# Batch 0 of a fused attention and mixer kernel: later panels and side blocks, a later z transpose, and relus shared between two engines

## The chip, the cores and the metric

The kernel runs on one core of a Trainium2 chip. The metric is the device time in microseconds (us) of one execution; lower is better. Engines are named as in the profile: PE is TensorE, PEld its weight load, DVE is VectorE, ACT is ScalarE, POOL is GpSimd, SP is SyncE, whose queue issues the transposing DMAs.

## The reference, cut to what matters

```python
scores = (1 / S) * z @ z.T             # 8 batches, S = 3136, z is S x 64
attn   = maximum(scores, 0) ** 2       # symmetric: scores of (o, j) and (j, o) are each other's transpose
x      = u * (attn @ v)                # D = 256
y      = x + (x.T @ U @ V).T           # rank 32
out    = y + maximum(y @ w1, 0) @ w2   # 256 -> 1024 -> 256
```

## The kernel before

S is cut into 25 tiles of 128. `A[j]` holds 13 of the 25 blocks of panel j; the other 12 blocks that an output o needs are the transposes of blocks in panel o itself, and come as a *strip* from one transposing DMA. So for every output tile o the order is: score matmul, relu with scale on ACT, square on DVE, transpose by DMA, and only then can PE use the strip. The *side blocks* of the start are those blocks of panels 8 to 15 that outputs 20 and later need.

```python
def score(b, parts):                        # parts: up to two pieces, each of at most 512 columns
    ps = pair_psum()                        # one PSUM tile of two banks
    ...                                     # one 64-row matmul per bank, the two side by side
    for dst, src in todo:
        nc.scalar.activation(out=dst, in_=src, func=AF.Relu, scale=sc)
    for dst, _ in todo:
        nc.vector.tensor_tensor(out=dst, in0=dst, in1=dst, op=ALU.mult)

def turn(b, o):                             # the strip; five buffers
    strip = strip_pool.tile([P, HALF, P], BF16, name="strip")
    transpose(out=strip, in_=A[o][:, P:])   # nc.sync.dma_start_transpose
    strips[b, o] = strip
```

Batches 1 to 7 find their panels half made by the batch before. Batch 0 finds nothing, so it has a start of its own: outputs 12 to 15 with half-made panels, then 16 to 19 (the "tail" of the start makes what is missing for outputs 20 and later), then the main loop over outputs 20, 21, 22, 23, 24, 0, 1, ... 11. The main loop calls an output "step i", where step 8 is output 20, step 12 is output 24, step 13 is output 0.

```python
# the start, cut
rest = []                                                    # side blocks for outputs 20 and later
for j in reversed(range(FIRST - NG, LEAD)):
    rest += score_steps(0, j, LEAD + NG - j, NB)             # 8 steps
more = [s for j in range(LEAD + NG, LEAD + 2 * NG - 1) for s in score_steps(0, j)]   # panels 20, 21, 22
for i, pair in enumerate(pairs):
    ...
    if B > 1 and i in (1, 2):                                # z of batch 1: doubled by DVE, turned by DMA
        part = ((0, FIRST), (FIRST, NF))[i - 1]
        double_z(1, (part,))
        turn_z(1, (part,))
    if i == len(pairs) - 1:
        turn(0, LEAD + NG)                                   # strip 20, in the same queue
...
# the main loop, cut: what is made in step i, and which strips are turned after it
first_at    = {8: [panel 23, panel 0], 9: [panel 24], 10: [panel 1, ...], 11: [panel 2, ...], 12: [...]}
first_turns = {8: (23,), 9: (24, 0)}                         # from step 10 on: the strip of step i + 4
```

Of the kernel before, what the change touches and what calls it, by code (L numbers as in the profile page):

```python
# [10 lines left out]
ALU = mybir.AluOpType  # L11
# [31 lines left out]
def kernel(  # L43
# [11 lines left out]
    nc = tc.nc  # L55
# [136 lines left out]
    def turn_z(b, parts):  # L192
        z_bf = z_tiles[b]
        for t0, t1 in parts:
            transpose(
                out=zT_of(b)[:, t0 : upto(t1), :],
                in_=z_bf[:, t0 : upto(t1), :, :].rearrange("p t h c -> p (t h c)"),
            )
# [90 lines left out]

    strips = {}  # L290

    def score(b, parts):

        ps = pair_psum()
        zT = zT_of(b)
        zT_flat = zT.rearrange("p t c -> p (t c)")
        for k, (j, c, n, _) in enumerate(parts):
            mm(  # L298
                out=ps[:, k, :n],
                lhsT=zT[halves[k], j, :],  # L300
                rhs=zT_flat[halves[k], c : c + n],
                start=True,
                stop=True,
            )
        if parts[0][3] is parts[-1][3]:
            n = parts[0][2]
            todo = [(parts[0][3], ps[:, :, :n] if len(parts) == 2 else ps[:, 0, :n])]
        else:
            todo = [(part[3], ps[:, k, : part[2]]) for k, part in enumerate(parts)]
        for dst, src in todo:  # L310
            nc.scalar.activation(out=dst, in_=src, func=AF.Relu, scale=sc)  # L311
        for dst, _ in todo:
            nc.vector.tensor_tensor(out=dst, in0=dst, in1=dst, op=ALU.mult)  # L313

    def score_steps(b, j, k0=0, k1=NB):
        steps = []
        n = (k1 - k0) * P
        parts = _ceil_div(n, 1024)
        each = n // parts
        h = each // 2  # L320
        for i in range(parts):
            at = k0 * P + i * each

            def step(at=at):
                dst = A[j][:, at : at + each].rearrange("p (i h) -> p i h", i=2)
                score(b, [(j, j * P + at + i * h, h, dst) for i in range(2)])

            steps.append(step)
        return steps
# [329 lines left out]
    def beside(o, j, w, stop=(False, False)):  # L659
        t0, _ = pair_of(o)  # L660
        for h in range(1 if j == NF else 2):
            half(0, o, j, h, w, (t0, h) not in begun, stop[h], skip_group_check=True)
            begun.add((t0, h))

    def start_up():
        parts = ((8, 16), (0, 8), (16, NF))
        first_z(parts[:2])
# [34 lines left out]
        where = {}  # L702
        mark = small.tile([P, D], BF16, name="mark", tag="t1_sb")[:1, :8]

        def make(pair):
            if all(LEAD - 1 - HALF <= j < FIRST for j in pair):
                todo = []
                for j in pair:
                    at = (FIRST - j) * P
                    where[j] = A[j][:, at : at + NG * P]  # L710
                    todo.append((j, c0, NG * P, where[j]))
                score(0, todo)
            else:
                room = rooms.pop(0)
                for i, j in enumerate(pair):
                    where[j] = room[:, i, :]
                score(0, [(j, c0, NG * P, room) for j in pair])

        def use(pair, some):
            for j in pair:  # L720
# [5 lines left out]
        for i, pair in enumerate(pairs):  # L726
            if i == 5 and B > 1:

                nc.sync.dma_start(out=mark, in_=v_both[1][:1, V_PARTS[2][1] - 1, :8])
            if i == 3:  # L730
                double_z(0, parts[2:])
            if i == 5:
                turn_on_pe([(16, NF)], [pair_psum().rearrange("p a w -> p (a w)")])
                turn_on_pe([(NF, NT)], [pair_psum()[:, 0, :]])
                extend_z(0)
            make(pair)
            if i > 5 and i % 2:
                nxt.pop(0)()
            if i > 1:
                use(pairs[i - 2], outs)  # L740
# [16 lines left out]
                    if 0 <= o - j <= HALF:  # L757
                        beside(o, j, block(0, o, j))

        def make_stored(pair):  # L760
            todo = []
            for j in pair:
                k0, k1 = LEAD - j, min(NB, LEAD + NG - j)
                todo.append((j, LEAD * P, (k1 - k0) * P, A[j][:, k0 * P : k1 * P]))
            score(0, todo)

        nxt += [lambda pair=pair: make_stored(pair) for pair in pairs[:2]]
        run(nxt[:2])
        own = [
            lambda j=j, some=some: use_stored([j], some)  # L770
# [2 lines left out]
            if j <= some[-1]  # L773
        ]
        run(_merge(nxt[2:], own))
        rest = []
        for j in reversed(range(FIRST - NG, LEAD)):
            rest += score_steps(0, j, LEAD + NG - j, NB)
        more = [s for j in range(LEAD + NG, LEAD + 2 * NG - 1) for s in score_steps(0, j)]
        for i, pair in enumerate(pairs):  # L780
            if i + 2 < len(pairs):
                make_stored(pairs[i + 2])
            else:
                more.pop(0)()
            use_stored(pair, outs)
            if B > 1 and i in (1, 2):
                part = ((0, FIRST), (FIRST, NF))[i - 1]
                double_z(1, (part,))
                turn_z(1, (part,))
            if i == len(pairs) - 1:  # L790
                turn(0, LEAD + NG)
        tail = []
        for o in outs:
            js = [(o + 1 + i) % NT for i in range(HALF)]

            def close(o=o, j=js[-1]):
                beside(o, j, block(0, o, j), [o % 2 == 1] * 2)
                if o % 2:
                    close_pair(0, o)
                if o == outs[1]:  # L800
                    load_u(0, LEAD + NG)
                if o < outs[-2]:
                    turn(0, o + NG + 1)

            for i in range(3):
                some = js[4 * i : min(4 * i + 4, HALF - 1)]
                tail.append(lambda o=o, js=some: [beside(o, j, block(0, o, j)) for j in js])
            tail.append(close)
# [8 lines left out]
    for j, i in enumerate((6, 7, 8, 9, 3, 5, 4, 2, 9, 8, 7, 6)):  # L817
        own_at[i].append((j, 0, FIRST - j))

    first_at = {8: [(NT - 2, 0, NB), (0, 0, NB)], 9: [(NT - 1, 0, NB)], 10: [(1, 0, NB)]}  # L820
    first_at.update({11: [(2, 0, NB)], 12: []})
    for j, i in zip(range(3, FIRST), (10, 11, 11, 12, 12, 12, 12, 12, 12)):
        first_at[i].append((j, 0, FIRST - j))
    first_turns = {8: (NT - 2,), 9: (NT - 1, 0)}

    next_at = {i: [] for i in range(NT)}
    for j in range(FIRST):
        next_at[max(NB, FIRST + j)].append((j, FIRST - j, NB))
    for j, i in enumerate((14, 15, 16, 18, 19, 20, 24)):
        next_at[i].append((FIRST + j, 0, NB))  # L830

    def run(steps):
        for s in steps:
# [6 lines left out]
    for b in range(B):  # L840
# [7 lines left out]
        for i in range(begin, NT):  # L848
            o = turns(i)
            fill = [s for key in own.get(i, ()) for s in score_steps(b, *key)]  # L850
            if more:
                fill += [s for key in next_at[i] for s in score_steps(b + 1, *key)]
                if b and i == 1:
                    load_z(b + 1, WHOLE)
                if b and i == 7:
                    turn_z(b + 1, ((FIRST, NF),))
                if b and i == 10:
                    turn_z(b + 1, ((0, FIRST),))
                if b == 0 and i in v_at:
                    load_v(b + 1, v_at[i])  # L860
                if i == 11:
                    extend_z(b + 1)
            main = attend_steps(b, o)
            if b and i in ahead:
# [80 lines left out]
```

## Time and profile before

| | before |
|---|---|
| time, median of 3 runs | 1003.15 us (999.58 to 1004.6) |
| span of the profiled run | 998.3 us |
| PE busy | 983.4 us |
| batch 0's own stretch (first attention matmul to the first of batch 1) | 94.2 us |

Two lines of the page of before: busy time by engine (first part) and the chain that ended last (fourth part).

```profile
PE 983.4 (99%) x13688; PEld 776.5 (78%) x13688; DVE 551.1 (55%) x1003; ACT 612.2 (61%) x835; POOL 171.7 (17%) x317
...
PE 91%; DVE 4%; ACT 3%; DMA 1%; issue 1%; POOL 0%; DVEq 0%; POOLq 0%
```

PE is nearly always busy and makes up 91% of the chain that ended last. There is little to gain except where PE is idle. The next view is the busy time of each engine in stretches of 10 us, with the granted PE clock, the share of the 16 DMA engines (packet time over the time of 16 engines, which can exceed 1) and GB/s.

```profile
core 0: us, PE busy (x) PEld busy (x) DVE busy (x) ACT busy (x) POOL busy (x), PEclk, DMA share, GB/s
20.00:30.00 10.00, 8.06 (x104) 5.46 (x103) 8.41 (x15) 9.51 (x15) 2.61 (x5) 1.00 1.03 179
40.00:50.00 10.00, 6.91 (x114) 5.58 (x111) 6.88 (x15) 7.38 (x13) 1.61 (x3) 1.00 1.19 200
60.00:70.00 10.00, 9.45 (x169) 6.70 (x166) 7.79 (x18) 7.61 (x16) 2.66 (x4) 1.00 1.22 208
70.00:80.00 10.00, 10.00 (x181) 8.54 (x176) 7.96 (x14) 8.01 (x11) 0.58 (x1) 1.00 1.30 204
80.00:90.00 10.00, 10.00 (x176) 8.37 (x172) 8.38 (x16) 7.84 (x11) 3.50 (x5) 1.00 1.18 186
```

PE has free time up to 70 us and none in the two rows after it. Which wait it is, the table of waits of PE between 16 and 95 us says (total us, how many, longest):

```profile
PE ps L371 <- DMA strip<-A: 2.5, 1, 2.5
PE ps L298 <- ACT A L311: 2.3, 4, 0.7
PE ps L371 <- DVE A L313: 2.0, 4, 0.9
```

The largest single wait is for a strip. Two lines of the queue's timeline and one of PE's show it. Columns: start, us, engine, line, operation, tiles, count, and in brackets the idle time before with what ended it.

```profile
38.59 3.33 SPq L195 DMA_TRANSPOSE zT<-z_bf  x2
42.02 24.05 SPq L333 DMA_TRANSPOSE strip<-A  x9
```

```profile
48.52 0.50 PE L371 MATMUL ps<-v,strip 64*128 64x256 bf16 x6 [2.48 <-DMA strip<-A]
```

Batch 1's two z turns were issued at 38.59 us, strip 20 behind them at 42.02, and PE sat 2.48 us until strip 20 had landed. Last, two lines of the groups by shape (busy us, mean ns | idle before), for the cost of a relu:

```profile
L311 ACT ACTIVATE A<-ps 128x1024 bf16<-128x1024 f32 x8 | 8.2, 1037 | 0.5 <-PE ps L298 0.5
...
L311 ACT ACTIVATE A<-ps 128x512 bf16<-128x512 f32 x12 | 6.7, 656 | 0.0
```

An ACT relu of 1024 columns takes 1037 ns and one of 512 takes 656 ns, both out of PSUM.

### The profile page before, as it was taken

Reading aid. Unit: us, or ns where it says so; the run is one execution under the profiler, and the core shown is the slowest. Engines: PE = TensorE matmul, PEld = TensorE weight load, DVE = VectorE, ACT = ScalarE, POOL = GpSimd, SP = SyncE. Lnnn points to the kernel's source line nnn. Section 1 sums busy time; section 2 is a strip of 40 time slices with the busy share of each in tenths; the row PEclk is TensorE's granted clock in tenths of the full one; section 3 lists DMA queues with packets and bytes.
Section 4 is the critical chain, followed back from the end, with each engine's and each line's share of the span. In section 5 each row is a group of like instructions: output and inputs, shape, how many; then the busy total and the mean of one; then the engine's idle time right before and its main releaser. Section 6 shows DMA issues by size and latency. Waiting matters only on the chain.

```text
span 998.3 us, 31020 instructions
## 1 busy us (share of the span) xinstructions
PE 983.4 (99%) x13688; PEld 776.5 (78%) x13688; DVE 551.1 (55%) x1003; ACT 612.2 (61%) x835; POOL 171.7 (17%) x317
## 2 busy tenths in 40 slices
PE   8899999999999999999999999999999999999998
PEld 6678777787778877788787887878877788787866
DVE  6878754467444665456644566445664457542352
ACT  8877764667645776466754667556674666643154
POOL 5111112111121211221112211112111120011000
PEclk9999999999999999999999999999999999999999
DMA  9999989899798999999999997989979998678533
GB/s 195 185 195 204 174 156 186 185 176 173 153 198 171 169 157 186 179 178 169 160 180 176 181 168 149 188 174 177 175 151 194 166 188 159 120 150 161 129 95 101
DMA packets 414790, 167.94 MB, mean 168 GB/s; under 512 B 389488, under 2 KB 399408, under 8 KB 414656
## 3 DMA queue, kind: packets, MB, share of 16 engines
q1 hardware_dynamic: 385424, 99.68, 62.3%
q0 software_dynamic: 29232, 66.28, 28.3%
q8 instruction: 107, 1.75, 0.7%
q14 instruction: 27, 0.22, 0.1%
HBM read 61.88 MB, written 25.69 MB: 88 GB/s over the span
## 4 chain that ended last, share of the span: by engine, by line
PE 91%; DVE 4%; ACT 3%; DMA 1%; issue 1%; POOL 0%; DVEq 0%; POOLq 0%
PE ps L371 47%; PE ps L563 17%; PE ps L610 17%; PE ps L298 6%; ACT A L311 2%; DVE A L313 2%; PE ps L405 1%; PE ps L531 1%; DVE x_bf L545 1%; DMA out_dram<-o_sb 1%; DMA strip<-A 1%; DVE both L386 1%; PE ps L479 1%; DVE x_bf L395 1%; PE ps L207 0%
## 5 line engine op out<-in xcount | busy, mean ns | idle before, releaser
L311 ACT ACTIVATE A<-ps 128x832 bf16<-128x832 f32 (+9 forms) x477 | 358.9, 769 | 155.4 <-PE ps L298 148.1
L371 PE MATMUL ps<-v,A 64*128 64x256 bf16 x4988 | 341.6, 269 | 1.8 <-DVE A L313 1.1
L313 DVE TENSOR_TENSOR A<-A 128x832 bf16<-128x832 bf16 (+9 forms) x477 | 244.7, 527 | 133.1 <-ACT A L311 130.0
L371 PE MATMUL ps<-v,strip 64*128 64x256 bf16 x4420 | 307.3, 269 | 3.4 <-DMA strip<-A 2.5
L371 PEld LDWEIGHTS <-A 64*128 64x128 bf16 x4988 | 246.3, 94 | 45.4 <-issue 10.0
L581 ACT ACTIVATE relu_bf<-ps 128x1024 bf16<-128x1024 f32 (+2 forms) x206 | 186.2, 911 | 140.0 <-PE ps L563 139.8
L371 PEld LDWEIGHTS <-strip 64*128 64x128 bf16 x4420 | 222.6, 94 | 37.2 <-DMA strip<-A 3.9
L624 DVE TENSOR_TENSOR o_sb<-ps,x_bf 128x512 f32<-128x512 f32 (+2 forms) x105 | 69.9, 665 | 243.7 <-PE ps L610 221.7
L610 PE MATMUL ps<-w_bf,relu_bf 128*128 128x256 bf16 (+1 forms) x1600 | 201.2, 273 | 0.0
L563 PE MATMUL ps<-ut,w_bf 128*128 128x512 bf16 (+2 forms) x896 | 198.6, 353 | 0.0
L610 PEld LDWEIGHTS <-relu_bf 128*128 128x128 bf16 (+1 forms) x1600 | 153.0, 98 | 45.6 <-issue 3.6
L563 PEld LDWEIGHTS <-w_bf 128*128 128x128 bf16 x896 | 84.9, 98 | 62.0 <-issue 6.9
L355 POOL DMA_DIRECT2D u_sb<-in_u_dram x96 | 53.7, 559 | 456.1 <-DVE x_bf L395 441.9
L298 PE MATMUL ps<-zT 64*128 64x416 bf16 (+8 forms) x812 | 131.6, 312 | 0.0
L385 ACT COPY both<-ps 128x512 f32<-128x512 f32 (+1 forms) x104 | 58.9, 566 | 72.9 <-PE ps L371 66.6
L637 POOL DMA_DIRECT2D out_dram<-o_sb x84 | 46.0, 548 | 276.2 <-DVE o_sb L624 272.9
L386 DVE TENSOR_TENSOR both<-ps,both 128x512 f32<-128x512 f32 (+1 forms) x104 | 69.3, 667 | 28.2 <-ACT both L385 27.5
L395 DVE TENSOR_TENSOR x_bf<-both,u_sb 128x512 bf16<-128x512 f32 (+1 forms) x104 | 69.8, 672 | 3.7
L545 DVE TENSOR_TENSOR x_bf<-ps,x_bf 128x512 bf16<-128x512 f32 (+1 forms) x112 | 65.5, 626 | 7.2 <-PE ps L531 7.1
L298 PEld LDWEIGHTS <-zT 64*128 64x128 bf16 x812 | 43.1, 94 | 4.0
L244 POOL DMA_DIRECT2D v<-in_v_dram x61 | 34.1, 561 | 0.8 <-DMA w_bf<-in_moe_w_ch_dram 0.7
L298 PE MATMUL ps<-relu_bf 64*128 64x416 bf16 (+9 forms) x121 | 22.2, 333 | 3.9 <-ACT A L311 3.3
(54 smaller groups left out, 208.0 us busy)
## 6 DMA issues: line engine op xcount, KB each, us to landing
u_sb<-in_u_dram POOLq DMA_DIRECT2D x96, 256.0 KB, 4.1
out_dram<-o_sb POOLq DMA_DIRECT2D x84, 256.0 KB, 3.3
v<-in_v_dram POOLq DMA_DIRECT2D x57, 192.0 KB, 4.8
strip<-A SPq DMA_TRANSPOSE x196, 5.5
out_dram<-o_sb SPq DMA_DIRECT2D x11, 256.0 KB, 2.0
z_c<-in_z_dram POOLq DMA_DIRECT2D x7, 384.0 KB, 5.9
u_sb<-in_u_dram POOLq DMA_DIRECT2D x16, 64.0 KB, 2.5
ut<-x_bf SPq DMA_TRANSPOSE x56, 3.7
```

The source lines that it names most:

```text
L298: mm(out=ps[:, k, :n], lhsT=zT[halves[k], j, :], rhs=zT_flat[halves[k], c : c + n], start=True, stop=True,)
L311: nc.scalar.activation(out=dst, in_=src, func=AF.Relu, scale=sc)
L313: nc.vector.tensor_tensor(out=dst, in0=dst, in1=dst, op=ALU.mult)
L371: mm(out=acc[t0][h][:, (o - t0) * D : (o - t0 + 1) * D], lhsT=w[halves[h]], rhs=v_both[b % 2][halves[h], j, :], start=start, stop=stop, **kw,)
L385: nc.scalar.copy(out=both[:, :w], in_=banks[1][:, :w])
L386: nc.vector.tensor_tensor(out=both[:, :w], in0=banks[0][:, :w], in1=both[:, :w], op=ALU.add)
L395: nc.vector.tensor_tensor(out=x_at(b, t0, n), in0=split(both[:, :w]), in1=u_sb[:, :n, :].rearrange("p t (a c) -> p t a c", c=P), op=ALU.mult,)
L545: nc.vector.tensor_tensor(out=q, in0=split(ps[h][:, : len(ks) * D]), in1=q, op=ALU.add)
L563: mm(out=ps[i][:, :w] if apart else ps[:, i, :w], lhsT=w1_bf[:, db, (hp + i) * P : (hp + i + 1) * P], rhs=uT[c][:, db, len(chunks[c]) * P ...
L581: nc.scalar.activation(out=relus[c][:, hp : hp + 2, :w], in_=ps[:, :, :w], func=AF.Relu)
L610: mm(out=ps[r, k * D : (k + 1) * D], lhsT=relus[c][:, ht, q : q + (TAIL if two else P)], rhs=w2_bf[:, ht, :], start=(ht < 1 + two), stop=( ...
L624: nc.vector.tensor_tensor(out=o_sb[:p].rearrange("p t (a c) -> p t a c", c=P), in0=split(ps[:p, k0 * D : (k + 1) * D]), in1=x_at(b, t, nk) ...
```

## The change

The intent: in the start PE waits for ACT and for strips, and after 70 us ACT has room. So (1) panel 22 leaves the crowded tail of the start for step 8, and panels 23, 24, 0, 1 and 2 are made one to three steps later than before, one a step; (2) the side blocks are made in pairs of panels, 10 of the 36 only in steps 9 and 10; (3) batch 1's z is turned in steps 10 and 11, so that strip 20 stands ahead of it; (4) in three score pairs of the start half of the relu goes to DVE. The diff, cut:

```diff
-    def score(b, parts):
+    def score(b, parts, shared=False):
...
+        relu = todo
+        if shared:
+            dst, src = todo[-1]
+            if len(todo) == 1:
+                dst, src = dst[:, 1, :], src[:, 1, :]
+                relu = [(todo[0][0][:, 0, :], todo[0][1][:, 0, :])]
+            else:
+                relu = todo[:1]
+            nc.vector.tensor_scalar(
+                out=dst, in0=src, scalar1=sc, scalar2=0.0, op0=ALU.mult, op1=ALU.max
+            )
-        for dst, src in todo:
+        for dst, src in relu:
             nc.scalar.activation(out=dst, in_=src, func=AF.Relu, scale=sc)
...
-            make(pair)
+            make(pair, i in (7, 9, 11))
...
-        rest = []
-        for j in reversed(range(FIRST - NG, LEAD)):
-            rest += score_steps(0, j, LEAD + NG - j, NB)
-        more = [s for j in range(LEAD + NG, LEAD + 2 * NG - 1) for s in score_steps(0, j)]
+        rest = [
+            lambda pair=pair: make_stored(pair, LEAD + NG)
+            for pair in zip(range(LEAD - 1, FIRST - NG, -2), range(LEAD - 2, FIRST - NG - 1, -2))
+        ]
+        more = [s for j in (LEAD + NG, LEAD + NG + 1) for s in score_steps(0, j)]
...
-            if B > 1 and i in (1, 2):
-                part = ((0, FIRST), (FIRST, NF))[i - 1]
-                double_z(1, (part,))
-                turn_z(1, (part,))
...
-    first_at = {8: [(NT - 2, 0, NB), (0, 0, NB)], 9: [(NT - 1, 0, NB)], 10: [(1, 0, NB)]}
-    first_at.update({11: [(2, 0, NB)], 12: []})
+    first_at = {8 + n: [(t, 0, NB)] for n, t in enumerate((22, 23, 24, 0, 1, 2))}
+    first_at[14] = []
...
+    first_more = {9: (LEAD - 1, LEAD - 2), 10: (LEAD - 3, LEAD - 4)}
-    first_turns = {8: (NT - 2,), 9: (NT - 1, 0)}
+    first_turns = {8: (22,), 9: (23,), 10: (24,), 11: (0,), 12: (1,), 13: (2, 3), 14: (4, 5)}
...                                           # batch 1's first panels: each two steps later, or one
+                if b == 0 and i == 9:
+                    double_z(b + 1, ((FIRST, NF), (0, FIRST)))
-                if b and i == 7:
+                if i == (7 if b else 10):
                     turn_z(b + 1, ((FIRST, NF),))
-                if b and i == 10:
+                if i == (10 if b else 11):
                     turn_z(b + 1, ((0, FIRST),))
-                if i == 11:
+                if i == (11 if b else 12):
                     extend_z(b + 1)           # a DVE copy that waits for z
```

No matmul is added or taken away.

More of the change, by code (lines that the diff above doesn't have):

```diff
@@ L663, in beside, with make_stored @@
             begun.add((t0, h))
+    def make_stored(pair, first, n=NG):
+        todo = []
+        for j in pair:
+            k0, k1 = first - j, min(NB, first + n - j)
+            todo.append((j, first * P, (k1 - k0) * P, A[j][:, k0 * P : k1 * P]))
+        score(0, todo)
     def start_up():
@@ L703, in start_up, with make @@
         mark = small.tile([P, D], BF16, name="mark", tag="t1_sb")[:1, :8]
-        def make(pair):
+        def make(pair, shared):
             if all(LEAD - 1 - HALF <= j < FIRST for j in pair):
@@ L711, in make @@
                     todo.append((j, c0, NG * P, where[j]))
-                score(0, todo)
+                score(0, todo, shared)
             else:
@@ L716, in make @@
                     where[j] = room[:, i, :]
-                score(0, [(j, c0, NG * P, room) for j in pair])
+                score(0, [(j, c0, NG * P, room) for j in pair], shared)
         def use(pair, some):
@@ L758, in use_stored @@
                         beside(o, j, block(0, o, j))
-        def make_stored(pair):
-            todo = []
-            for j in pair:
-                k0, k1 = LEAD - j, min(NB, LEAD + NG - j)
-                todo.append((j, LEAD * P, (k1 - k0) * P, A[j][:, k0 * P : k1 * P]))
-            score(0, todo)
-        nxt += [lambda pair=pair: make_stored(pair) for pair in pairs[:2]]
+        nxt += [lambda pair=pair: make_stored(pair, LEAD) for pair in pairs[:2]]
         run(nxt[:2])
@@ L775, in start_up @@
         run(_merge(nxt[2:], own))
-        rest = []
-        for j in reversed(range(FIRST - NG, LEAD)):
-            rest += score_steps(0, j, LEAD + NG - j, NB)
-        more = [s for j in range(LEAD + NG, LEAD + 2 * NG - 1) for s in score_steps(0, j)]
+        rest = [
[3 more added lines that the diff above has]
+        more = [s for j in (LEAD + NG, LEAD + NG + 1) for s in score_steps(0, j)]
         for i, pair in enumerate(pairs):
             if i + 2 < len(pairs):
-                make_stored(pairs[i + 2])
+                make_stored(pairs[i + 2], LEAD)
             else:
@@ L801, in close @@
                     load_u(0, LEAD + NG)
-                if o < outs[-2]:
-                    turn(0, o + NG + 1)
+                    turn(0, LEAD + NG + 1)
             for i in range(3):
@@ L818 @@
         own_at[i].append((j, 0, FIRST - j))
-    first_at = {8: [(NT - 2, 0, NB), (0, 0, NB)], 9: [(NT - 1, 0, NB)], 10: [(1, 0, NB)]}
-    first_at.update({11: [(2, 0, NB)], 12: []})
-    for j, i in zip(range(3, FIRST), (10, 11, 11, 12, 12, 12, 12, 12, 12)):
+    first_at = {8 + n: [(t, 0, NB)] for n, t in enumerate((22, 23, 24, 0, 1, 2))}
+    first_at[14] = []
+    for j, i in zip(range(3, FIRST), (10, 11, 12, 13, 14, 14, 14, 14, 14)):
         first_at[i].append((j, 0, FIRST - j))
-    first_turns = {8: (NT - 2,), 9: (NT - 1, 0)}
+    first_more = {9: (LEAD - 1, LEAD - 2), 10: (LEAD - 3, LEAD - 4)}
+    first_turns = {8: (22,), 9: (23,), 10: (24,), 11: (0,), 12: (1,), 13: (2, 3), 14: (4, 5)}
     next_at = {i: [] for i in range(NT)}
@@ L830 @@
         next_at[i].append((FIRST + j, 0, NB))
+    after_first = {i: [] for i in range(NT)}
+    for j in range(FIRST):
+        after_first[max(NB + 1, FIRST + j)].append((j, FIRST - j, NB))
+    for j, i in enumerate((16, 17, 18, 20, 21, 22, 24)):
+        after_first[i].append((FIRST + j, 0, NB))
     def run(steps):
@@ L850 @@
             fill = [s for key in own.get(i, ()) for s in score_steps(b, *key)]
+            if b == 0 and i in first_more:
+                fill.append(lambda pair=first_more[i]: make_stored(pair, LEAD + 2 * NG))
             if more:
-                fill += [s for key in next_at[i] for s in score_steps(b + 1, *key)]
+                coming = next_at if b else after_first
+                fill += [s for key in coming[i] for s in score_steps(b + 1, *key)]
                 if b and i == 1:
                     load_z(b + 1, WHOLE)
-                if b and i == 7:
+                if b == 0 and i == 9:
+                    double_z(b + 1, ((FIRST, NF), (0, FIRST)))
+                if i == (7 if b else 10):
                     turn_z(b + 1, ((FIRST, NF),))
-                if b and i == 10:
+                if i == (10 if b else 11):
                     turn_z(b + 1, ((0, FIRST),))
```

## The prediction

> **What bounds the kernel.** TensorE. The profile's first part has it busy 983.4 of 998.3 us; the chain that ended last is 91% PE. The table by stretches of 10 us shows PE at 10.00 in nearly every one after 70 us; before that 7.78, 8.99, 8.06, 9.94, 6.91, 9.09, 9.45. "Busy" flatters it: paired 256-column half-row matmuls start 0.107 us apart, and at that rate I estimate the PE work between 16 and 68 us as 38 us, so 14 are lost there, of which 2 are the loss of any stretch. That is all that this change can reach: it alters batch 0 alone, and takes no matmul away.
>
> **Where the loss is.**
> 1. 18–25 us: ScalarE takes 1.04 us for a pair's 1024 columns (groups by shape), PE about 1.07; where an extra panel step comes in, ScalarE is last. About 2 us.
> 2. 36–44 us (the start's tail): ScalarE evicts almost without a pause, PE's estimated work is 6 of 8 us.
> 3. 46.0–48.5 us: the waits show PE idle 2.48 us on "DMA strip<-A". The transposes leave SP in order: batch 1's two z turns (issued at 38.59 and 40.13, landing at 42.8 and 46.0) stand ahead of strip 20 (issued 42.02, landing 48.47). The Trainium skill, "DMA: Bandwidth & Descriptors", "Silent corruption: two transposing streams in flight at once", says why they share one stream; this trace has all on SP.
> 4. 57 us: 0.91 us before panel 22's last matmul. The profile names DVE, but strip 23 landed then (57.51).
> 5. 62–65 us (panel 24): five narrow side steps in a row; about 1 us on ScalarE.
>
> **What the change does.**
> - Three pairs' relus are halved: ScalarE 1.04 to 0.66 us (its 512 form), VectorE gains about 0.67 each (its 512-column PSUM operations; the skill, "VectorE: DVE Perf Modes", "Why PSUM operands drop a tier", says fp32 from PSUM runs at 1x). VectorE is already 84% busy: I count 0.5 us.
> - Panel 22 and 10 of 36 side blocks leave the start's tail: 12 score steps become 6. A pair of panels needs two activations (0.66 each, against 1.04 for one of 1024), yet ScalarE loses about 2.5 us there. Gain 1.5–2 us.
> - z turned at steps 10 and 11: strip 20 is no longer late. Gain 2.5 us.
> - Panel 24's fills fall from 6 to 3: gain 0.5–1 us.
> - Against it: panels 22, 23, 24, 0, 1 are made and turned two steps ahead or less. Strips land 4–6 us after issue (median 5.9 here); a step is 3.5–4 us. Strip 23, turned after step 9, is read at the end of step 10 (block 24 of the pair's second output): I expect a wait of 1–2 us there, up to 1 us at strips 24 and 0, with the z turns between them. New waits together about 2 us.
>
> Sum: 0.5 + 2 + 2.5 + 0.7 − 2 = about 4 us gained, all on the critical path, because PE is short of work only there. After 110 us nothing should change.
>
> **Predicted: 999 us, 80% range 995 to 1003; faster by over 2%: 0.01, within 2%: 0.98, slower: 0.01.**
>
> **What would show it.** PE idle before 70 us falls from 10 to about 6 us; the 2.48 us strip wait near 46 us is gone; ScalarE's busy time in 30–45 us falls; a new strip wait (DMA, or DVE misnamed) of 1–2 us at the end of panel 22, at 52–55 us; panel 24 about 1 us shorter.
>
> **What would make it wrong.** Strip waits of 2 us each for 22, 23, 24, 0 would eat everything (1002–1004). If strips land in 4 us once z is out of the way, the gain is 5–6 us (997). The runs of before span 5 us, so luck moves the median as much as the change.

## The result, and the profile after

| | before | after |
|---|---|---|
| median | 1003.65 us (4 runs) | 1013.04 us (4 runs, 1011.24 to 1014.85) |
| ratio | | 1.0101, 95% interval 1.0064 to 1.0139 |

A ratio here is the mean time of one kernel's fast runs over that of the other's fast runs of the same rounds, so it is not quite the ratio of the medians. A later set of runs gave 1.0077 (1.0043 to 1.0111), median 1010.04 us. The change cost 7 to 10 us; it had been predicted to save 4.

The page of after, the same two lines as of before:

```profile
PE 986.5 (97%) x13684; PEld 779.2 (77%) x13684; DVE 553.8 (55%) x1010; ACT 611.2 (60%) x839; POOL 171.2 (17%) x317
...
PE 86%; DMA 6%; DVE 5%; ACT 2%; issue 0%; POOL 0%; SPq 0%; DVEq 0%; POOLq 0%
```

PE's share of the chain fell from 91% to 86% and DMA's rose from 1% to 6%. The stretches of 10 us, with the same columns as before:

```profile
20.00:30.00 10.00, 7.40 (x104) 5.44 (x101) 7.35 (x12) 7.68 (x11) 2.42 (x5) 1.00 1.05 169
40.00:50.00 10.00, 8.32 (x132) 6.69 (x132) 5.49 (x14) 6.58 (x13) 0.54 (x1) 1.00 1.15 166
60.00:70.00 10.00, 8.85 (x159) 6.46 (x155) 5.69 (x12) 6.89 (x11) 1.09 (x2) 1.00 1.20 212
70.00:80.00 10.00, 6.49 (x114) 5.42 (x108) 5.82 (x15) 5.86 (x12) 1.08 (x2) 1.00 0.98 154
80.00:90.00 10.00, 9.19 (x132) 7.30 (x134) 6.69 (x12) 6.05 (x9) 0.56 (x1) 0.83 1.04 169
```

PE is now idle up to 90 us, not 70, and in the last row the granted clock is 0.83. The waits of PE between 16 and 95 us:

```profile
PE ps L382 <- DMA strip<-A: 7.9, 5, 2.6
PE ps L298 <- ACT A L322: 5.2, 8, 1.7
PE ps L382 <- DVE A L324: 1.1, 3, 0.5
```

7.9 us on strips in five waits, where before had 2.5 in one. This profiled run of after was a bad one at its start, where two of the five waits lie (1.93 and 0.73 us; see the slow stretches in the last section). A second trace of after, whose time was 1009.67 us, has a cleaner picture, which a third repeats (4.1 us on strips in the same two places):

```profile
PE ps L298 <- ACT A L322: 5.2, 9, 1.2
PE ps L382 <- DMA strip<-A: 4.2, 2, 2.1
PE ps L382 <- DVE A L324: 1.1, 3, 0.5
```

To see where time goes, I counted attention matmuls in the traces: every output has 49, so the start of each output can be told, whatever is interleaved. The table has the length of each stage in us, for two traces of before and three of after; "lost" is the length less an estimate of PE's work, made from the 0.107 us that 256 columns took at full clock in the trace of before.

| stage | before | before, 2nd | after | after, 2nd | after, 3rd | lost: before | lost: after, 2nd |
|---|---|---|---|---|---|---|---|
| start to the first strip | 27.60 | 29.82 | 32.48 | 30.37 | 30.61 | 6.24 | 9.01 |
| tail (outputs 16 to 19) | 8.57 | 8.58 | 7.09 | 6.28 | 6.28 | 2.01 | 0.34 |
| output 20 | 6.02 | 6.10 | 3.53 | 3.29 | 3.28 | 2.72 | 0.33 |
| output 21 | 3.08 | 2.98 | 3.24 | 3.24 | 3.24 | 0.12 | 0.10 |
| output 22 | 4.39 | 3.32 | 5.61 | 7.05 | 7.31 | 1.19 | 3.77 |
| output 23 | 3.59 | 3.58 | 3.39 | 3.97 | 3.76 | 0.23 | 0.79 |
| output 24 | 4.22 | 4.22 | 2.97 | 2.85 | 2.85 | 2.36 | 1.01 |
| output 0 | 2.72 | 2.72 | 6.25 | 4.65 | 4.66 | 0.02 | 1.53 |
| output 1 | 3.16 | 3.16 | 3.71 | 3.71 | 3.71 | 0.12 | 0.53 |
| output 2 | 3.08 | 3.08 | 6.02 | 5.07 | 4.99 | 0.02 | 2.35 |
| outputs 3 to 11 | 27.72 | 27.72 | 29.59 | 29.13 | 29.28 | 0.66 | 1.37 |
| batch 0's stretch | 94.2 | 95.3 | 103.9 | 99.6 | 100.0 | 15.7 | 21.1 |
| batches 1 to 7 and the end | 896.3 | 896.2 | 900.5 | 900.4 | 898.3 | | |

The start of the second trace of before has a wait of 1.86 us for the first strip in it, that of the first trace of after one of 1.93 us; without these, the start took 27.60 and 27.96 us in before and 30.37 to 30.61 us in after.

The estimated PE work of the stretch is 78.5 us in both, so the difference of 5.4 us between the first column and "after, 2nd" is lost time. The gains that were wanted are there: tail, output 20 and output 24 lose 5.4 us less. The losses are larger: the start (2.8), outputs 22 and 23 (3.1), outputs 0 to 2 (4.2), the rest (0.7). For each the traces show at least a part of the cause.

**The shared relus run one after the other.** Three lines of the timeline of after:

```profile
19.78 0.68 DVE L318 TENSOR_SCALAR A<-ps 128x512 bf16<-128x512 f32 x1
...
20.50 2.27 ACT L322 ACTIVATE A<-ps 128x512 bf16<-128x512 f32 x3 [1.36 <-DVE A L318]
...
21.15 0.39 PE L298 MATMUL ps<-relu_bf 64*128 64x512 bf16 x2 [0.73 <-ACT A L322]
```

ACT's half of the pair starts at 20.50, behind the end of DVE's half (19.78 + 0.68), and ACT, the busier engine here, was idle 1.36 us for it. This is no accident of the schedule: in the trace each of the three ACT halves waits for the semaphore that DVE's half increments. I had costed 0.66 us for both halves together; in the trace they take 1.32 us (19.78 to 21.10), more than the 1.04 of one engine alone.

The two halves are read from one PSUM tile of two banks. The mixer of this same kernel shares relus too, but from two PSUM tiles of one bank each, into one SBUF tile. There the two engines overlap, in 18 of 18 places in the trace of before, as in these two lines of its timeline:

```profile
121.02 0.69 DVE L571 TENSOR_SCALAR relu_bf<-ps 128x512 bf16<-128x512 f32 x1 [0.44 <-PE ps L563]
121.51 0.59 ACT L579 ACTIVATE relu_bf<-ps 128x512 bf16<-128x512 f32 x1
```

So a common SBUF tile does not force the order. The common PSUM tile as the reason fits both cases, but no run took it away from the scores.

**Strip 22 is late, then strip 2.** In the second and third trace the wait in output 22 is 2.0 and 2.1 us, the one in output 2 is 2.1 both times. In the second, strip 22 was issued at 48.97 us and landed at 55.47; PE had asked for it at 53.51.

**DVE stands before a copy that waits for z.** Four lines of after, output 0:

```profile
68.29 0.56 DVE L238 COPY zT<-zT 128x1536 bf16<-128x1536 bf16 x1 [1.62 <-DMA zT<-z_bf]
...
70.31 0.42 DVE L397 TENSOR_TENSOR both<-ps,both 128x256 f32<-128x256 f32 x1
...
70.76 0.82 ACT L402 COPY both<-both 64x256 f32<-64x256 f32 x2 [3.06 <-DVE both L397]
...
72.52 0.34 PE L298 MATMUL ps<-relu_bf 64*128 64x384 bf16 x2 [1.73 <-ACT A L322]
```

DVE took its instructions in the order of the program. The copy of zT, which step 12 now issues, waited 1.62 us for z's turn; the squares and output 24's sum (70.31) stood behind it, ACT's next copy waited 3.06 us for that sum, and PE lost 1.73 us to ACT.

The second and third trace differ: z had landed (at 63.14 us in the second) before the copy began, DVE did not stop, and PE still lost 1.25 and 1.08 us there. Two lines of the second:

```profile
64.80 0.55 DVE L238 COPY zT<-zT 128x1536 bf16<-128x1536 bf16 x1
...
69.01 0.34 PE L298 MATMUL ps<-relu_bf 64*128 64x384 bf16 x2 [1.25 <-ACT A L322]
```

The copy's own 0.55 us and three squares stood ahead of output 24's sum, and ACT waited 1.35 us for that sum with the next relu behind it. So the stop for z is only a part of this loss, and in the first trace alone.

**The clock fell.** Three stretches of 3.4 us around 81.7 us:

```profile
78.30:81.70 3.40, 0.89 (x17) 0.80 (x19) 0.31 (x1) 0.83 (x2) 0.00 (x0) 1.00 1.17 166
81.70:85.10 3.40, 3.40 (x36) 2.45 (x32) 3.24 (x6) 1.30 (x3) 0.56 (x1) 0.50 1.01 201
85.10:88.50 3.40, 3.40 (x64) 2.83 (x60) 1.68 (x4) 2.50 (x5) 0.00 (x0) 1.00 1.35 188
```

After a stretch with 0.89 us of PE busy the granted clock was 0.50 for 3.4 us. None of the traces of before shows this before the kernel's end.

### The profile page after: what moved, and what is told of

The parts are those of the page before. It is cut to its first block, busy times and chain, and to the rows that moved or that the text cites. A ratio compares the mean times of both kernels' runs of the same rounds, so it can differ in the third digit from the quotient of the medians.

```text
span 1012.8 us, 31020 instructions
## 1 busy us (share of the span) xinstructions
PE 986.5 (97%) x13684; PEld 779.2 (77%) x13684; DVE 553.8 (55%) x1010; ACT 611.2 (60%) x839; POOL 171.2 (17%) x317
## 4 chain that ended last, share of the span: by engine, by line
PE 86%; DMA 6%; DVE 5%; ACT 2%; issue 0%; POOL 0%; SPq 0%; DVEq 0%; POOLq 0%
PE ps L382 43%; PE ps L574 17%; PE ps L621 17%; PE ps L298 6%; DMA zT<-z_bf 3%; DMA strip<-A 3%; DVE A L324 2%; ACT A L322 1%; DVE x_bf L556 1%; PE ps L416 1%; PE ps L542 1%; DMA z_c<-in_z_dram 1%; DVE both L397 1%; PE ps L490 1%; DVE x_bf L406 1%
## 5 line engine op out<-in xcount | busy, mean ns | idle before, releaser
L322 ACT ACTIVATE A<-ps 128x832 bf16<-128x832 f32 (+10 forms) x481 | 358.1, 761 | 162.4 <-PE ps L298 147.3
L324 DVE TENSOR_TENSOR A<-A 128x832 bf16<-128x832 bf16 (+10 forms) x481 | 245.1, 524 | 135.3 <-ACT A L322 132.0
```

## The experiments

Each set was run with before on the same chip, and ratios are to those runs. In all, before had a median of 1002.77 us in 55 such runs, and about one run in seven, of any kernel, stood 4 to 13 us above the median of its kernel. Medians are therefore given beside the ratios.

The kernels were made from one source with a switch for each of the three parts; with all switches off and on its compiled instructions were the same as those of before and after.

In short: no part of the change shows a gain by itself. Of the parts alone, the later panels with the side blocks, and the side blocks by themselves, are slower with an interval that leaves out 1; for the relus and the late z the traces show new waits, and the times don't decide. The last column is batch 0's stretch in the one profiled run of each kernel.

| kernel | ratio to before | batch 0's stretch, us |
|---|---|---|
| before | | 94.2, 95.3 |
| after | 1.0101, 1.0077 | 103.9, 99.6, 100.0 |
| shared relus | 1.003 | 95.6 |
| shared relus, ACT first | 0.9992 | 94.6 |
| later panels and side blocks | 1.009 | 105.1 |
| later panels and side blocks, idle matmuls | 1.0125 | 106.0 |
| side blocks | 1.0034 | 96.1 |
| late z | 1.0024 | 97.1 |
| later panels, side blocks and late z | 1.0041 | 100.1 |
| the same, zT's copy later | 1.0027 | 98.1 |
| the same, more lead | 1.0035 | 98.2 |
| the same, both | 1.0038 | 104.8 (slow stretch) |
| z in the gaps | 0.9999, 0.9995 | 93.5, 93.8 |
| z in the gaps, second turn later | 1.0013 | 98.4 (slow stretch) |
| the same with side blocks | 0.9996 | 93.5 |
| z in the gaps, v later | 0.9969 | 92.0 |

### Each part alone

Only the shared relus (panels and z as before):

```diff
-            make(pair)
+            make(pair, i in (7, 9, 11))
```

> Kernel before plus the three shared relus alone. Theory A (the two halves of a shared relu run one after the other: in the trace of after ScalarE sits idle 1.36 us before its half until VectorE's half ends): about 2 us slower than before, ratio 1.002, and ScalarE waits on VectorE's relu three times in 17 to 28 us. Theory B (the halves run side by side, the loss is only elsewhere): 0.5 us faster, no such wait.

Measured: median 1005.26 us, before 1002.41, ratio 1.003 (0.9991 to 1.0069). The time alone doesn't decide. The trace does: ACT's relus between 16 and 29 us in this kernel,

```profile
L326 ACT ACTIVATE A<-ps 128x832 bf16<-128x832 f32 (+2 forms) x12 | 9.3, 841 | 3.9 <-DVE A L322 3.9
```

with 3.9 us of idle time, all ended by DVE's half, and the start takes 30.95 us where before took 27.60 and, without its wait for a strip, 27.96. So theory A has the mechanism. Its cost of 2 us is not shown: the interval holds 1, and in the trace most of the start's delay is made up again, because strip 20 still lands when it lands behind z. PE waited 0.60 us for it where before waited 2.48, output 20 took 4.32 us instead of 6.02, and batch 0's stretch was 95.6 us, against 94.2 and 95.3.

Only the later panels and paired side blocks (z turned early):

> Kernel before plus the later panels and paired side blocks, with the z turns of batch 1 left early. Theory A (short lead between making a panel and needing its strip, two steps instead of four): 3 to 6 us slower than before, strip waits at panels 22, 0 and 2 of 1 to 2.6 us each, besides the old 2.5 us wait on strip 20. Theory B (the late z turns among the strips are what delays them): within 2 us of before, no strip waits after 55 us.

Measured: median 1013.08 us, ratio 1.009 (1.0064 to 1.0116), so as much as the loss of after with one part of the change. Its waits on strips:

```profile
PE ps L386 <- DMA strip<-A: 7.8, 5, 3.6
PE ps L420 <- DMA strip<-A: 2.6, 1, 2.6
```

They are 3.57 us for strip 20 and 2.23 us for strip 21 (which the last matmul of output 20's step reads), 2.57 us in output 24 and 1.62 us in output 2. The first two are not of panels made late: strips 20 and 21 stand behind z's turns as in before, PE comes to them sooner, and with the side blocks alone, where no panel is made late (further down), the same two waits are 2.43 and 1.98 us. Outputs 20 and 21 took 10.95 and 4.86 us, against 6.02 and 3.08, which is 6.7 of the 11.0 us by which batch 0's stretch is longer. The short lead shows in the waits on strips 24 and 2. No z turn stands among these, so theory B, which had no strip wait after 55 us, falls; theory A had a smaller loss and named 22, 0 and 2, of which only 2 came. The clock, in stretches of 3.4 us:

```profile
46.60:50.00 3.40, 1.85 (x18) 1.21 (x20) 0.00 (x0) 0.00 (x1) 0.34 (x1) 0.51 1.32 228
50.00:53.40 3.40, 1.23 (x11) 0.56 (x7) 0.59 (x1) 0.86 (x1) 0.00 (x0) 0.50 1.12 142
53.40:56.80 3.40, 3.34 (x31) 2.38 (x33) 0.59 (x1) 0.86 (x1) 0.00 (x0) 0.50 0.42 78
56.90:60.30 3.40, 3.40 (x57) 3.00 (x54) 1.90 (x4) 2.92 (x5) 0.00 (x0) 1.00 0.13 26
```

It fell to half and stayed there for three windows, from 46.6 to 56.8 us, so PE lost more than the waits by themselves.

Only z late:

> Kernel before plus the late z turns alone (doubling at step 9, turns at steps 10 and 11, batch 1's first panels two steps later); panels and their turns as before. Theory A (short lead is the cause): 1 to 3 us faster than before, the 2.5 us wait on strip 20 near 46 us gone and no new strip waits above 1 us. Theory B (z among the strips is the cause): 2 to 6 us slower, new strip waits between 58 and 82 us, and VectorE held up at the copy of zT until z lands.

Measured: median 1004.65 us, ratio 1.0024 (0.9991 to 1.0058). The wait on strip 20 is gone (output 20 takes 3.37 us), as theory A had it, but the gain isn't:

```profile
PE ps L302 <- DMA zT<-z_bf: 2.8, 1, 2.8
...
PE ps L386 <- DMA strip<-A: 1.0, 2, 0.6
```

Now it is z itself that is late: its second half stood in the queue behind strips 24, 0 and 1, landed at 69.41, and PE waited 2.8 us for it, followed by 3.4 us at half clock. Neither theory had PE wait for z itself. B had one thing right: DVE stood 7.56 us before the copy of zT until z had landed. But the new strip waits that B expected did not come (1.0 us in two waits), so its main point falls here too.

Later panels and late z together, without the shared relus:

> Kernel after without the shared relus. If the shared relus cost 2 us as the trace suggests: about 7 to 8 us slower than before, ratio 1.007 to 1.008, and the late strip waits and the half clock stay as in after. If they cost nothing: as after, ratio 1.010.

Measured: median 1006.84 us, ratio 1.0041 (1.0006 to 1.0076): less than expected, and less than half the cost of the later panels alone (1.009), because strip 20 no longer stands behind z. The strip waits in outputs 22, 0 and 2 (1.48, 1.10 and 2.06 us), the stop at zT (1.64) and the half clock (76.2 to 79.6 us) are all there. What remains to after is not told apart by these times, whose intervals overlap, and the traces don't put it on the relus: without them the start is about 2 us shorter (28.53 us, against 30.37 and 30.61), but batch 0's stretch is 100.1 us, against 99.6 and 100.0.

After again, in a later set:

> Kernel after once more, beside the parts. As measured at first: ratio 1.010 (10 us slower). If the shared relus cost only their own 2 us on top of panels and z late (1.0041): ratio 1.006. If they also push the strips into slower transposes: 1.010 again.

Measured: median 1010.04 us, ratio 1.0077 (1.0043 to 1.0111). This lies between the two expectations and, with these intervals, decides neither. Its trace has no slow strips at the tail, so nothing there speaks for a further effect of the relus.

### Which of the two later things: side blocks or panels?

Only the side blocks later in pairs; the panels as before:

```diff
-        rest = []
-        for j in reversed(range(FIRST - NG, LEAD)):
-            rest += score_steps(0, j, LEAD + NG - j, NB)
+        rest = [ make_stored(pair, LEAD + NG) for the four pairs ]   # as in the change
+    first_more = {9: (LEAD - 1, LEAD - 2), 10: (LEAD - 3, LEAD - 4)}
```

> Kernel before with the side blocks alone made later in pairs; panels, their turns, z and relus as before. Theory (short lead of the panels is the cause, the side blocks are harmless): within 1.5 us of before, ratio 0.9985 to 1.0015, strip waits as before. Rival (moving ScalarE work behind the start is itself bad): 3 us slower or more.

Measured: median 1005.73 us, ratio 1.0034 (1.0008 to 1.0059), so the expectation of "harmless" missed. The trace says why: the tail did shrink (7.47 us from 8.57), but PE only came sooner to strips 20 and 21, which land when they land behind z: it waited 2.43 and 1.98 us there, and output 20 took 8.44 us. What ACT had gained went into a wait on the transposing queue. Batch 0's stretch is 96.1 us, against 94.2 and 95.3, so this explains at most 1.9 us; the later batches took 899.9 us in this trace (see below).

### The clock

Later panels alone with idle matmuls before strips 20 and 22, to keep the clock up:

```diff
+            if b == 0 and i in (8, 10):
+                main.insert(13, lambda n=16 if i == 8 else 10: keep_busy(n))   # n matmuls of 512 columns
```

> Later panels alone, with 16 and 10 idle matmuls of 512 columns (3.4 and 2.1 us at full clock) put where PE waits for strips 20 and 22. Theory (a long gap lets the clock fall to half, and that is a good part of the loss): no half clock before 60 us, 3 to 4 us faster than the later panels alone, so 6 to 7 us slower than before. Rival (the clock doesn't matter, the waits are all): the same 10 us slower, or worse by what the idle matmuls overrun.

Measured: median 1016.97 us, ratio 1.0125: slower than without. The idle matmuls did keep the clock at full speed up to 54.7 us, but then PE waited 3.08 us for strip 21 at the end of output 20's step, where it had waited 2.23 us without them, and the clock fell there. So the wait and the fall only moved, and the run says nothing on what the clock costs.

The traces give a rule instead. Over all 20 traces PE's idle time was added up in each window of 3.413 us, the unit in which the granted clock changes, counted from the first clock record of the trace. In all 16 cases in which the clock fell within the kernel, PE had been idle for 1.92 to 3.41 us of the window before. In windows at full clock after which it didn't fall, the most was 1.86 us. Once the clock was at half, less idle time kept it there: it stayed after six windows with 0.55 to 2.23 us, and rose after sixteen with 0 to 0.42 us. The 2.48 us wait of before straddled two windows (1.12 and 1.36 us) and didn't do it; the 2.01 us wait in the second trace of after lay in one and did. The Trainium skill, "TensorE: Matmul & The Clock Gate", section "What's actually happening", has the free-running window of 3413 ns, and the traces agree (the first clock record stands 4.1 to 7.0 us after the start of the span, and the spells between changes are multiples of 3.413 us); but its section "Why this matters for your kernels" asks for no gaps over about 3 us, which is too generous.

### The relus, with the order turned round

```diff
-            nc.vector.tensor_scalar(...)            # DVE's half first
-        for dst, src in relu:
-            nc.scalar.activation(...)
+        for dst, src in relu:
+            nc.scalar.activation(...)               # ACT's half first
+        if shared: nc.vector.tensor_scalar(...)
```

> Shared relus alone, with ScalarE's half put ahead of VectorE's (so VectorE waits for ScalarE instead of the other way round). Theory (the program orders the two reads of one PSUM tile, and with VectorE first ScalarE, the busier of the two, stands still 1.4 us): the 2 to 3 us of the shared relus shrink to under 1 us, ratio 0.999 to 1.001, the stretch before the first strip about 28 us instead of 30.9. Rival (VectorE's added work is the cost): 1.003 again.

Measured: median 1002.42 us, before 1002.23, ratio 0.9992 (0.9963 to 1.0021). The two times are not told apart, and this interval overlaps that of DVE's half first; what is gone is the wait. First the ACT relus of after between 16 and 28 us, then those of this kernel between 16 and 29:

```profile
L322 ACT ACTIVATE A<-ps 128x832 bf16<-128x832 f32 (+2 forms) x10 | 7.6, 835 | 3.9 <-DVE A L318 3.9
```

```profile
L323 ACT ACTIVATE A<-ps 128x832 bf16<-128x832 f32 (+2 forms) x14 | 11.2, 847 | 2.0 <-PE ps L302 1.9
```

ACT doesn't wait for DVE any more (idle 2.0 us, nearly all for PE), the start takes 28.74 us where it took 30.95 with DVE first. So the added work on DVE was affordable, and the order made the longer start. There is no gain either: the halves still don't run side by side, DVE's now begins when ACT's has ended (16.27 after 16.24 us in the first pair).

### Lead and the stop at zT

Later panels and late z, with zT's copy moved behind step 13:

```diff
-                if i == 12: extend_z(1)          # before output 24's step
+            if i == 13: extend_z(1)              # behind output 0's step
```

> Later panels and late z (1.0041 as measured) with VectorE's copy that extends batch 1's zT moved from before panel 24's step to after panel 0's step. Theory (VectorE, in order, stands 1.6 us before that copy until z has landed, and holds up the squares, then ScalarE, then PE): PE's 1.6 us gap on ScalarE behind panel 0 is gone, 1.5 to 3 us faster than later panels and late z, ratio about 1.002. Rival (VectorE's stop is harmless, strip 0 is what matters): 1.004 again.

Measured: median 1005.68 us, ratio 1.0027 (0.9992 to 1.0061). In the trace output 0 takes 4.19 us instead of 6.24, and PE's gap on ACT there shrinks from 1.64 to 0.69 us; the rest is the wait on strip 0 (1.10 us), which this trace doesn't have. The strip wait in output 2 stays (2.12 us). The times are not told apart (1.0041 before it), so the cost of the copy and its stop is shown by the trace alone, and 0.69 us of the gap is of neither.

Later panels and late z, with one step more of lead (22 and 23 both in step 8, 24 in 9, 0 in 10, 1 in 11, 2 in 12, and the turns with them):

> Later panels and late z with one step more between making and use for panels 23, 24, 0, 1, 2 (panels 22 and 23 both made in step 8). Theory (the short lead makes the strip waits): the waits on strips 0 and 2 (1.1 and 2.1 us) and the half clock are gone, ratio 0.999 to 1.001. Rival (the transposing queue is simply full once z stands among the strips): waits stay, ratio 1.003 to 1.005.

Measured: median 1005.62 us, ratio 1.0035 (1.0 to 1.0071). In the trace the waits on strips 0 and 2 are gone as the theory has it: outputs 0 and 2 take 2.79 and 2.75 us, against 6.24 and 6.30. But the time isn't better, and as to time the expectation failed. Strip 22, which gained no lead, still made PE wait 1.72 us, the clock fell there, and the stop at zT moved to output 1 (1.93 us).

Both of these together:

> Later panels, late z, one step more of lead, and VectorE's copy of zT after panel 0's step: both suspected costs taken away. Theory (short lead and VectorE's stop are all of batch 0's loss but the relus): ratio 0.998 to 1.001, no PE gap over 1 us on ScalarE or strips between 58 and 85 us. Rival (something else in the later panels costs): 1.003 or more.

Measured: median 1007.09 us, ratio 1.0038 (1.0004 to 1.0072), with runs from 1001.9 to 1011.53. Outputs 0, 1 and 2 take 2.79, 3.98 and 2.73 us in the trace, so the two costs are gone where they were; output 22 keeps its 1.69 us wait and the half clock. The profiled run then fell into a slow stretch of the DMA: strip 3 was issued at 67.00 us and landed at 80.02, PE waited 4.94 us, and the clock was at half for 10.2 us. The strips issued in 56 to 68 us, and then those in 68 to 80 us (count, median us from issue to landing):

```profile
strip<-A SPq DMA_TRANSPOSE x4, 6.7
```

```profile
strip<-A SPq DMA_TRANSPOSE x3, 11.3
```

Whether short lead and zT are *all* of the cost can't be told from so few runs with such stretches in them. Shown is that the strip waits in outputs 0 and 2 are gone from the trace with more lead, and that the gap on ACT in output 0 shrinks when the copy is moved.

### A better version: only z, and in another place

The trace of late z alone shows the transposing queue idle behind strip 22 (44.5 to 48.3 us) and behind strip 23 (50.1 to 52.5). So: before, with the z turns put there, panels and relus untouched.

```diff
                 double_z(1, (part,))
-                turn_z(1, (part,))
...
                     turn(0, o + NG + 1)
+                if o == outs[1]:                   # behind strip 22
+                    turn_z(1, ((0, FIRST),))
...
                 for t in first_turns[i]:
                     turn(b, t)
+                if i == 8:                         # behind strip 23
+                    turn_z(1, ((FIRST, NF),))
```

> Kernel before with the two z turns moved to where the transposing queue stands idle: one behind strip 22, one behind strip 23, before strips 24 and 0. Theory (the order in the one transposing queue decides; strip 20 must not stand behind z): the 2.5 us wait on strip 20 is gone, no new wait over 1 us, 2 to 3 us faster than before, ratio 0.997 to 0.998. Rival (the DMA engines are full there, and the wait only moves): within 1 us of before, a wait of 1 to 2 us on strip 23, 24 or on z.

> The two z turns in the gaps of the transposing queue, again, to see through the outlier of the first time. 2 us faster than before in the median, ratio 0.997 to 0.999 where no run stands out.

Measured in two sets: medians 1000.84 and 1000.94 us, before 1002.74 and 1002.23; ratios 0.9999 and 0.9995, each with one run (1013.5 and 1010.14) far above the other five. Output 20 takes 3.37 us, as wanted, but there is a wait on strip 23 of 1.13 and 1.48 us, which the second trace of before doesn't have (the first has 0.91 us there). Both theories were half right: part of the wait was saved, part moved.

With z's second turn one step later, and the same with the side blocks in pairs:

> Kernel before with z's first turn behind strip 22 and its second behind strips 24 and 0 (step 9). Theory (z's second turn crowded strip 23): the 1.1 to 1.5 us wait for strip 23 at the end of panel 22 shrinks below 0.8 us, 2 to 3 us faster than before in the median, ratio 0.997 to 0.999. Rival (loads of u and v crowd it, not z): the wait stays, as with the turns in the gaps before: 1 to 2 us faster in the median.

> The same with the side blocks made later in pairs. Theory (alone they cost only because strips 20 and 21 stood behind z when the start's tail got shorter): 1 us faster than the same without, ratio 0.996 to 0.998. Rival (they cost by themselves): slower than the same without, by 1 to 3 us.

Measured: medians 1004.49 and 1002.62 us, before 1002.77; ratios 1.0013 and 0.9996. In both the wait on strip 23 stayed (2.16 and 1.49 us), so z's second turn isn't what delays it. No cost of the side blocks can be seen once strips 20 and 21 stand ahead of z (the tail is 7.38 us, and no wait in outputs 20 and 21). The first of the two had a slow stretch of the DMA from about 80 to 84 us in its trace.

Last, z in the gaps and batch 1's loads of v begun at step 12 instead of step 9:

```diff
-        v_at = dict(zip((9, 11, 13, 15, 18, 21), V_PARTS[3:]))
+        v_at = dict(zip((12, 14, 16, 18, 20, 22), V_PARTS[3:]))
```

> z's turns in the gaps, and batch 1's v loads begun at step 12 instead of step 9 of batch 0. Theory (loads crowd the strips): strip 23 lands 1 us or more earlier after its issue than the 7.6 us it took, the 1.1 to 1.5 us wait at the end of panel 22 falls under 0.5 us, and the kernel is 1 us faster than with z in the gaps alone, about 999.5 to 1000 us where before has 1002.5. Rival (the transposes are slow by themselves): the wait stays and the time is 1000.9 as before.

Measured: median 999.71 us, before 1002.8, ratio 0.9969 (0.9933 to 1.0005): the lowest median, though its interval just holds 1, so a gain over before is likely rather than shown. Its waits of PE between 16 and 95 us:

```profile
PE ps L302 <- ACT A L326: 2.6, 5, 0.7
PE ps L386 <- DVE A L328: 1.1, 3, 0.5
PE ps L386 <- DMA strip<-A: 0.4, 1, 0.4
```

Strip 23 landed 6.1 us after its issue instead of 7.6, the wait at the end of output 22 is gone and output 22 takes 3.26 us. That fits loads of v crowding the strip, in one trace of this kernel and two of z in the gaps. The Trainium skill, "DMA: Bandwidth & Descriptors", section "Issuing engines are not separate DMA queues", says that DMAs of all issuing engines run on the same 16 DMA engines; this agrees with it.

### Batches 1 to 7

> The kernel before, for a second trace. If batches 1 to 7 vary by themselves: their stretch (896.3 us in the first trace) differs by 1 us or more here, with waits on output stores in other places. If they don't: 896.3 us within 0.5.

> The kernel after, for a third trace. If batches 1 to 7 are slower because of the change: 900 us or more for them again. If they vary by themselves: anything from 895.5 to 900. Batch 0 in either case about 3 to 6 us longer than in before.

Measured: 896.2 us for before (896.3 in its first trace), 898.3 us for after (900.5 and 900.4). Their instructions there are the same. PE's waits of over 0.3 us there sum to 2.3 to 3.6 us in after and to 0.3 and 0.5 us in before, all on DVE; in one of them (1.34 us at 287 us in the second trace) DVE had waited for an output store. Other kernels had 895.7 (z in the gaps) to 899.9 us (side blocks only), and up to 905.9 (more lead), where PE waited 3.9 us at 654 us and the clock fell. Later panels and late z, which is after without the relus, had 897.1. So part of it varies by itself. Whether a part comes from the change stays open; it is 4 of the 9.5 us by which the second trace of after is longer than the first of before.

## Why the prediction was wrong, point by point

- *PE bounds the kernel, and all that can be gained or lost lies before 70 us.* The first half held. The second didn't: after loses time up to 95 us, and 2 to 4 us more in later batches, of which the cause is open.
- *Shared relus: gain 0.5 us.* Wrong step: "ScalarE 1.04 to 0.66 us" took it that the halves run side by side. They are ordered by a semaphore, ACT waited 3.9 us in three places, and the start grew by 2 to 3 us. Turning the order round took that away.
- *Start's tail: gain 1.5 to 2 us.* Right: 8.57 to 6.28 us. Of the 2.3 us, 0.6 is PE work that only moved.
- *Strip 20 no longer late: gain 2.5 us.* Right: its stage lost 2.4 us less.
- *Panel 24: gain 0.5 to 1 us.* Right, somewhat more: 1.4 us.
- *New strip waits: together about 2 us.* This is the term of the sum that was mis-sized most, and placed wrongly. Expected were 1 to 2 us on strip 23 and up to 1 us on 24 and 0. Measured were 2.0 to 2.1 us on strip 22, and 2.1 us on strip 2, in two traces, and 7.9 us in all in the first (2.7 of it at the start); strips 23 and 24 hardly made PE wait. I had set the lead of each strip against a landing time of 4 to 6 us, where the trace of before has 3.6 to 9.8 (8.0 for strip 22), and forgot that gains upstream bring PE to the strip sooner: in before strip 22 landed at 54.78 us and PE asked for it at 54.94, with 0.16 us to spare; in the second trace of after it landed at 55.47, and PE asked at 53.51.
- *Not in the sum at all:* the fall of the clock (half clock for 3.4 us in each trace of after, and 13.7 us in the later panels alone) and the gap on ACT in output 0 (1.1 to 1.7 us of PE), of which DVE's stop before zT's copy is a part in the first trace alone.
- *What would make it wrong: strip waits of 2 us each would eat everything.* That was the right worry with too small a limit (1004 us), because the waits bring the clock down with them.

The sum of batch 0 for the second trace: gains 1.7 + 2.4 + 1.4, losses 2.8 + 3.1 + 4.2 + 0.7, net a loss of 5.4 us where 4 us of gain had been predicted.

## What to carry to other kernels

A stage that looks bound by one engine may hand its gain straight to the next queue: before moving work later, compare for each consumer the time at which it will *now* ask with the time at which its DMA lands, and count idle time of about 2 us or more within one clock window of 3.4 us (1.92 us was enough here) as costing more than its length. When two engines are to share one result, look in the compiled program or the trace for a semaphore between them before costing them as parallel. An engine that takes its instructions in order, as DVE did here, holds up everything behind a copy that waits for a DMA, so such a copy is issued as late as its reader allows.

## What the Trainium skill lacked or had wrong

- "TensorE: Matmul & The Clock Gate", "Why this matters for your kernels": it asks for no PE gaps over about 3 us. Here 1.92 us of idle time within one window of 3.413 us was enough (16 of 16 falls at 1.92 to 3.41 us), and 1.86 us wasn't; a wait of 2.48 us across two windows did no harm. In these traces the idle time within a window decided, not the length of a gap. The page has no figure for the idle time that keeps the clock at half: here 0.55 us in a half-clock window did, and 0.42 us didn't.
- "PSUM — Partial Sum Buffer", "Specifications (TRN2)": it says that ScalarE and VectorE can access PSUM in parallel as long as banks don't collide. From two tiles of one bank each they did (18 of 18 shared relus of the mixer in the trace of before overlap). Within one tile no run here had them do so: the program orders the two reads of its two banks, with 1.23 to 1.36 us of ACT idle time per pair. No page warns of that.
- "DMA: Bandwidth & Descriptors" has no word on stretches of some us in which all transfers are slow. In one trace (later panels, late z, more lead and the later copy) 60 to 76 GB/s were moved from 72 to 78 us where 270 were moved in the 2 us before, and strips took 11.3 us in the median to land instead of 6.7. Such a stretch was also in the first trace of after at 31 to 40 us (strip waits of 1.93 and 0.73 us). Their cause is open.
- "DMA: Bandwidth & Descriptors" has bandwidths of transposes but no time from issue to landing under load. Here a transpose of 12 blocks of 128x128 landed after 3.7 to 10.2 us, median 6.0, in the first trace of after.
